# Keeping five transposed K units of batch 0 on chip, lending the wq buffer to the load ring, and turning the q projection round, in a two-layer decode kernel on one core

## The chip, the core and the metric

The kernel runs on one core of one Trainium2 chip. The metric is the time of one execution in microseconds (us) of device time; lower is better. A time is the median of several runs with the lowest and highest beside it. "Span" is the length of one profiled execution, which is 1.5 to 3 us shorter than the time. The ratios given with the times are the mean time of one kernel's fast runs over that of the kernel before in the same rounds, with a 95% interval, so they are not quite the ratio of the medians quoted. By the 2% bar of the record all kernels here are "same" (run 1: "unclear"); "slower" and "faster" below mean only that the interval excludes a ratio of 1.

Words used throughout: PE is TensorE's matmul, PEld its weight load, DVE is VectorE, ACT is ScalarE, SP or SPq the engine (its queue) that issues the loads. L62 is line 62 of that kernel's file. The *granted clock* is the share of TensorE's full speed that the throttle let through. The *DMA share* is the mean busy share of the 16 DMA engines, which can come out a little over 1. A *unit* is 1 MiB of the K or V cache: two chunks of 2048 rows of one head of one batch, 128 x 4096 bf16 on chip. A *slot* is a buffer for one unit.

## The reference, cut to what matters

Two attention layers and two MLPs on one token per batch. **Both layers use the same K and V cache and the same weights.**

```python
# B = 4, D = 512, Hq = 32, Hkv = 8, Sk = 8192, Dh = 128, F = 1792, all bf16
def attn(x, k_cache, v_cache, wq, wo):
    q = (x @ wq).reshape(B, 1, Hq, Dh).transpose(0, 2, 1, 3)
    k, v = jnp.repeat(k_cache, 4, axis=1), jnp.repeat(v_cache, 4, axis=1)
    p = softmax(einsum("bhqd,bhkd->bhqk", q, k) * Dh ** -0.5)
    o = einsum("bhqk,bhkd->bhqd", p, v)
    return o.transpose(0, 2, 1, 3).reshape(B, 1, Hq * Dh) @ wo

x = x + attn(layernorm(x), ...)
x = x + (silu(n @ w_gate) * (n @ w_up)) @ w_down      # n = layernorm(x)
x = x + attn(layernorm(x), ...)                       # layer 2: the same caches
x = x + (silu(n @ w_gate) * (n @ w_up)) @ w_down
```

K and V are 64 units each, and each is wanted in two layers: 256 uses of a unit. A use whose unit is still in a slot from layer 1 needs no load.

## The kernel before

A small planner inside the kernel decides the order of all instructions. Loads are issued by SP in one fixed order, given as a string. `a` loads a V unit for layer 1 (all 64 have one); `b` loads it again for layer 2; `c` stands in place of `b` where the unit **stays in its slot** until layer 2 has used it, and is no load; `K` is the next K unit of the K sequence; the rest are weights. The place of a token also sets the priority of the work on its unit. The three digits are batch, head and half.

```python
ORDER = ("K c241 c230 K x a061 c201 c021 c310 c240 K c110 c100 c101 c311 a021 K wq K c000 c020 wo3 c001 K K K "
         ...
         "b220 b321 b251 b340 b341 b370 b371 b320 b350 b351 b360 b361 ")
NSLOT = 11
NLATE = 3
...
KSEQ = [(0, 0), (0, 1), (1, 0), (0, 2), (1, 1), (0, 3), (1, 2), (1, 3)]   # (layer, batch)
```

A load takes the slot that comes free first, and waits on SP until then. A slot comes free when the matmul that used the unit last has ended. Every K unit gets two transposes on VectorE, in place, before its 32 score matmuls:

```python
def k_pair(u, ld, prio, prev):
    _, l, b, g, cp = u
    for h in range(2):
        def t(h=h):
            ap, key = unit_ap(u, h)
            v = ap.bitcast(mybir.dt.uint32)
            op("dve", lambda e: e.transpose(v, v), reads=[key], writes=[key])
        tr.append(PL.add("dve", 1.23, t, [ld], prio))
    ...                                        # 32 matmuls with the transposed K moving, into banks 0 to 3
    st = PL.add("pe", 1.95, qk, tr + [qd, prev] + (scores_free[0] or []), prio, n=64)
    st.slot_of = u                             # its end frees the slot
```

Between the layers each batch has a chain: output projection, layer norm, MLP, layer norm, then the query of layer 2 in two halves of 16 heads. Here `wq` is stationary and the four columns of x move, in 64 small matmuls a half:

```python
def q_proj(heads, deps, tag):
    ...
    for h in heads:
        for kt in range(KT):
            op("pe", lambda e: e.matmul(ps[:, bk * BW + h * B:bk * BW + (h + 1) * B],
                                        lhsT=wq_sb[:, kt, h * Dh:(h + 1) * Dh],
                                        rhs=xnT[:, kt * B:(kt + 1) * B], ...))
...
for hf in range(2):
    mm = q_proj(range(hf * Hq // 2, (hf + 1) * Hq // 2), [cen, mm], tag)   # 2nd half after the 1st
    out_.append(q_half(b, hf, tag, [mm, qs], prior))                      # scale, spread, place in qpad
```

No score of layer 2 of a batch can run before its query. The V product of most heads is already written in the turned-round form (probabilities stationary, V moving, four 32-column tiles side by side), followed by a 128x256 transpose in PSUM; the last three heads (`NLATE`) are written in a direct form.

## Time and profile before

| Measure | Before |
|---|---|
| Time, median of 4 runs beside the changed kernel | 642.83 us (642.42 to 643.32) |
| Profiled span, mean granted clock | 641.5 us, 0.685 |
| Loads of 1 MiB for K and V | 232 (128 K, 104 V; 24 V uses need none) |
| Read from HBM | 257.17 MB |
| Busy: DVE / PE / ACT | 421.6 / 418.5 / 40.2 us |
| Last landing to the end | 11.2 us |

The prediction below shows the page, the stretches and the chain at the hole. One more view carries the argument: the end of the chain of waits, whose columns are start in us, length in us, and what it was.

```profile
610.92 19.43 DMA pool<-in_A_v_cache_dram
...
630.39 1.03 PE ps L705 x32
```

The last load is issued at 610.92 us, lands at 630.35, and what follows (32 matmuls of the last V unit, output projection, layer norm, MLP) takes to the end of the span and has no load beside it.

I took the DMA rate in stretches of 4 us from 0 to 624 us and summed length x (1 - rate/420), where 420 GB/s is what undisturbed stretches show. The sum of a segment is the time that it lost against that rate, as if nothing had been read for so long. One load of 1 MiB is 1.0486 MB / 420 GB/s = 2.5 us.

| Losses in us, before | 0-140 | 140-168 | 168-200 | 200-280 | 280-340 | 340-540 | 540-572 | 572-624 | sum |
|---|---|---|---|---|---|---|---|---|---|
| | 3.9 | 1.6 | 2.6 | -0.1 | 1.3 | 1.5 | 1.9 | 0.0 | 12.6 |

### The profile page before, as it was taken

The page shows a single profiled execution, that of the slowest core. Times are in us where ns is not written, and L with a number is a line of the kernel's source. Part 1 is how long each engine was busy: PE and PEld are TensorE (multiplying, and loading weights), DVE is VectorE, ACT ScalarE, POOL GpSimd, SP SyncE. Part 2 cuts the span into 40 slices and gives each one's busy share as a digit, 9 for nine tenths or more (in the row PEclk, how much of TensorE's full clock was granted, in tenths as well). Part 3 has the DMA queues.
Part 4 walks back from the last instruction along what each step waited for, and adds up shares of the span by engine and source line. Part 5 has one row for each costly group of instructions (what it writes and reads, how often), then busy time and mean ns, then how long its engine had stood idle before and what let it go on. Part 6 is the DMA issues. An engine that isn't in the chain of part 4 may idle for free.

```text
span 641.5 us, 18860 instructions
## 1 busy us (share of the span) xinstructions
PE 418.5 (65%) x8721; PEld 210.1 (33%) x8721; DVE 421.6 (66%) x740; ACT 40.2 (6%) x106; POOL 1.8 (0%) x8
## 2 busy tenths in 40 slices
PE   0276455656677676578775675777666776876765
PEld 0231131215532242235322242224522254622355
DVE  5278864745289979565686976576487763599722
ACT  1000200003000100000200100000200020000200
POOL 1000000000000000000000000000000000000000
PEclk9995676776576789766577686565676675578675
DMA  8999999999999999999999999999999999999991
GB/s 359 411 417 420 407 419 421 406 413 382 403 369 419 421 420 419 420 420 398 415 411 421 420 417 421 420 412 421 404 403 421 418 422 419 393 398 422 420 418 68
DMA packets 41127, 258.39 MB, mean 403 GB/s; under 512 B 3924, under 2 KB 9816, under 8 KB 10840
## 3 DMA queue, kind: packets, MB, share of 16 engines
q1 hardware_dynamic: 41048, 257.19, 97.8%
q8 instruction: 68, 1.11, 0.7%
q14 instruction: 11, 0.09, 0.0%
HBM read 257.17 MB, written 0.00 MB: 401 GB/s over the span
## 4 chain that ended last, share of the span: by engine, by line
DMA 60%; PE 18%; DVE 15%; SPq 4%; issue 2%; ACT 1%
DMA pool<-in_A_k_cache_dram 34%; DMA pool<-in_A_v_cache_dram 26%; DVE pool L568 8%; PE ps L580 7%; PE ps L720 5%; SPq L92 4%; DVE negm L598 2%; PE ps L460 1%; DVE ps L739 1%; PE ps L758 1%; DVE pp L627 1%; PE ps L638 1%; PE ps L683 1%; PE ps L811 1%; DVE osum L741 1%
## 5 line engine op out<-in xcount | busy, mean ns | idle before, releaser
L568 DVE STREAM_TRANSPOSE pool<-pool 128x1024 uint32<-128x1024 uint32 x256 | 303.4, 1223 | 69.0 <-DMA pool<-in_A_k_cache_dram 62.2
L580 PE MATMUL ps<-pool,qpad 32*32 32x512 bf16 x4096 | 229.4, 528 | 84.6 <-DVE pool L568 82.0
L580 PEld LDWEIGHTS ps<-pool,qpad 32*32 32x32 bf16 x4096 | 67.3, 107 | 220.6 <-DVE pool L568 155.0
L720 PE MATMUL ps<-pool,pp 128*32 128x256 bf16 x1952 | 98.2, 352 | 60.5 <-DMA pool<-in_A_v_cache_dram 47.3
L720 PEld LDWEIGHTS ps<-pool,pp 128*32 128x32 bf16 x1952 | 54.6, 116 | 100.5 <-DMA pool<-in_A_v_cache_dram 67.9
L739 DVE STREAM_TRANSPOSE ps<-ps 128x256 f32<-128x256 f32 x61 | 27.9, 457 | 68.9 <-PE ps L720 68.9
L602 ACT ACTIVATE pp<-ps,negm 128x512 bf16<-128x512 f32 x32 | 21.6, 685 | 336.4 <-DVE negm L598 249.2
L683 PE MATMUL ps<-oT,wo_sb 128*128 128x4 bf16 x640 | 22.8, 166 | 15.4 <-DVE oT L743 10.9
L460 PE MATMUL ps<-xnT,wq_sb 128*128 128x4 bf16 x640 | 18.4, 166 | 19.2 <-DMA wq_sb<-in_A_wq_dram 17.5
L683 PEld LDWEIGHTS ps<-oT,wo_sb 128*128 128x128 bf16 x640 | 20.2, 102 | 28.9 <-DVE oT L743 19.1
L598 DVE TENSOR_REDUCE negm<-ps 128x1 f32<-128x512 f32 x32 | 19.8, 679 | 13.0 <-PE ps L580 13.0
L460 PEld LDWEIGHTS ps<-xnT,wq_sb 128*128 128x128 bf16 x640 | 17.6, 103 | 21.0 <-DMA wq_sb<-in_A_wq_dram 17.6
L638 PE MATMUL ps<-ident,pp 128*128 128x128 bf16 x128 | 14.9, 293 | 9.5 <-DVE pp L627 8.8
L638 PEld LDWEIGHTS ps<-ident,pp 128*128 128x128 bf16 x128 | 11.9, 137 | 14.9 <-DVE pp L627 10.8
L446 ACT ACTIVATE lnv<-var,eps_sb 128x4 f32<-128x4 f32 x10 | 3.0, 297 | 219.3 <-DVE var L441 219.3
L741 DVE TENSOR_REDUCE osum<-ps 128x4 f32<-128x32 f32 x61 | 11.7, 191 | 2.1
L743 DVE TENSOR_TENSOR oT<-osum,invL 128x4 bf16<-128x4 f32 x61 | 10.3, 169 | 2.1
L705 PE MATMUL ps<-pp,pool 128*128 128x4 bf16 x192 | 5.9, 167 | 6.5 <-DMA pool<-in_A_v_cache_dram 6.5
L647 ACT ACTIVATE pp<-ps 128x1024 bf16<-128x1024 bf16 x8 | 8.2, 1024 | 23.9 <-PE ps L638 23.9
L627 DVE TENSOR_SCALAR pp<-pp,alpha 128x512 bf16<-128x512 bf16 x32 | 9.0, 343 | 1.1 <-ACT alpha L620 1.1
L758 PE MATMUL ps<-xnT,wg_sb 128*128 128x4 bf16 x280 | 8.2, 166 | 2.1 <-DVE xnT L435 1.5
L811 PE MATMUL ps<-hT,wd_sb 128*128 128x4 bf16 x280 | 8.5, 166 | 1.1 <-DVE hT L803 0.6
(61 smaller groups left out, 126.7 us busy)
## 6 DMA issues: line engine op xcount, KB each, us to landing
pool<-in_A_k_cache_dram SPq DMA_DIRECT2D x128, 1024.0 KB, 9.6
pool<-in_A_v_cache_dram SPq DMA_DIRECT2D x104, 1024.0 KB, 10.7
wq_sb<-in_A_wq_dram SPq DMA_DIRECT2D x1, 4096.0 KB, 24.0
wo_sb<-in_A_wo_dram SPq DMA_DIRECT2D x4, 1024.0 KB, 18.0
wu_sb<-in_B_w_up_dram SPq DMA_DIRECT2D x2, 896.0 KB, 13.9
wg_sb<-in_B_w_gate_dram SPq DMA_DIRECT2D x2, 896.0 KB, 15.9
wd_sb<-in_B_w_down_dram SPq DMA_DIRECT2D x2, 896.0 KB, 12.4
pp<-in_A_x_dram SPq DMA_DIRECT2D x1, 4.0 KB
```

The source lines that it names most:

```text
L92: ins = self.eng[engname].dma_start(out_ap, in_ap)
L460: op("pe", lambda e: e.matmul(ps[:, bk * BW + h * B:bk * BW + (h + 1) * B], lhsT=wq_sb[:, kt, h * Dh:(h + 1) * Dh], rhs=xnT[:, kt * B:(kt ...
L568: op("dve", lambda e: e.transpose(v, v), reads=[key], writes=[key])
L580: op("pe", lambda e: e.matmul(ps[32 * c:32 * (c + 1), a * BW:(a + 1) * BW], lhsT=qpad[rows, qbuf, es_, g, :], rhs=ap[h][rows, :, es_ // 2, ...
L598: op("dve", lambda e: e.tensor_reduce(negm[:, q, a:a + 1], bank(a), AX.X, ALU.max, negate=True), reads=[f"pb{a}"], writes=[f"negm{q}_{a}"])
L602: op("act", lambda e: e.activation(pblk(q)[:, :, a, :], bank(a).rearrange("p (t j) -> p t j", j=32), ACTF.Exp, bias=negm[:, q, a:a + 1], s ...
L627: op("dve", lambda e: e.tensor_scalar(seg, seg, alpha[:, q, a:a + 1], None, op0=ALU.mult), reads=[f"pp{q}_{a}", f"alpha{q}"], writes=[f"pp ...
L638: op("pe", lambda e: e.matmul(stg[:, t * P:(t + 1) * P], lhsT=pp[:, q, blk * P:(blk + 1) * P], rhs=ident[:], is_transpose=True, start=True ...
L683: op("pe", lambda e: e.matmul(ps[:, OPJ * BW + nq * B:OPJ * BW + (nq + 1) * B], lhsT=wo_sb[:, h, nq * P:(nq + 1) * P], rhs=oT[:, l, h, :], ...
L720: op("pe", lambda e: e.matmul(ps[32 * n:32 * (n + 1), bk * BW:bk * BW + 256], lhsT=pp[:, q, col:col + 32], rhs=v[:, 8 * f:8 * (f + 1), 32 ...
L739: op("dve", lambda e: e.transpose(blk, blk), reads=[f"pb{bk}"], writes=[f"pb{bk}"])
L741: op("dve", lambda e: e.tensor_reduce(osum[:], diag, AX.X, ALU.add), reads=[f"pb{bk}"], writes=["osum"])
```

## The change

Its intent: (1) keep the last five transposed K units of batch 0's layer 1 in their slots, so that layer 2 of batch 0 needs neither load nor transpose for them and can score as soon as its query is there; (2) hand the `wq` buffer (four units long) to the load ring as four more slots once the last query is projected; (3) project the query with x stationary and `wq` moving, four 32-column tiles side by side, 16 matmuls a half; (4) load the last unit in two halves, so that half of its matmuls run before the last landing; (5) a new load order, in which batch 0 keeps no V unit (before 6) and batches 1 to 3 keep 6, 5 and 7 (before 6 each). Besides, the K units of a batch come in another order of heads, and the step lengths that the planner assumes were set anew, so that the order of all instructions differs.

```diff
+            for i in range(s.gives):
+                slots.append((s.end + self.HOP, self.nslots + i))
...
-NLATE = 3
+LATE = (6, )
+KM = (5, 0, 0, 0)
+TAILSPLIT = True
...                                               (the order string is replaced)
+        def q_rows(hf, deps, tag):
+            nh = Hq // 2
+            def mm():
+                bk = pbk(tag)
+                for kt in range(KT):
+                    w = wq_sb[:, kt, hf * nh * Dh:(hf + 1) * nh * Dh].rearrange("p (h d) -> p h d", d=Dh)
+                    for n in range(4):
+                        op("pe", lambda e: e.matmul(ps[32 * n:32 * n + B, bk * BW:(bk + 1) * BW],
+                                                    lhsT=xnT[:, kt * B:(kt + 1) * B],
+                                                    rhs=w[:, :, 32 * n:32 * (n + 1)],
+                                                    start=(kt == 0), stop=(kt == KT - 1), tile_position=(0, 32 * n)),
...                                               (in q_half)
-                src = ps[:, bass.ds(bk * BW + b + hf * nh * B, nh, step=B)]
+                blk = bank(bk).bitcast(mybir.dt.uint32)
+                op("dve", lambda e: e.transpose(blk, blk), reads=[f"pb{bk}"], writes=[f"pb{bk}"])
+                src = ps[:, bass.ds(bk * BW + b, nh, step=32)]
...
+        def slot_sb(s):
+            return pool[:, s, :] if s < NSLOT else wq_sb[:, s - NSLOT, :]
...                                               (in load_pair: the last unit in two loads)
+            return [PL.load(1.25, lambda: half(0), u), PL.load(1.25, lambda: half(1), None)]
...                                               (in k_pair)
-            for h in range(2):
+            for h in range(2 if ld is not None else 0):
...
-            st.slot_of = u
+            if u not in kept_k:
+                st.slot_of = home[u]
...                                               (in the chain)
-                mm = q_proj(range(hf * Hq // 2, (hf + 1) * Hq // 2), [cen, mm], tag)
+                mm = q_rows(hf, [cen, mm], tag)
                 out_.append(q_half(b, hf, tag, [mm, qs], prior))
+            if b == B - 1:
+                mm.gives = KT
...                                               (in the load loop)
-                loads[u] = load_pair(u)
+                if u[1] == 1 and ("k", 0) + u[2:] in kept_k:
+                    home[u] = ("k", 0) + u[2:]
+                else:
+                    loads[u] = load_pair(u)
```

## The prediction

> **What bounds the kernel now.** I read the page's first four parts first, then the stretches (rate of the DMA engines, 4 us at a time over the whole span), then the chain of waits and the DMA queue's own waits around each dip.
>
> From the page: engine totals, two of the rows in 40 slices, DMA queue, chain.
>
> ```profile
> PE 418.5 (65%) x8721; PEld 210.1 (33%) x8721; DVE 421.6 (66%) x740; ACT 40.2 (6%) x106; POOL 1.8 (0%) x8
> ...
> DMA  8999999999999999999999999999999999999991
> GB/s 359 411 417 420 407 419 421 406 413 382 403 369 419 421 420 419 420 420 398 415 411 421 420 417 421 420 412 421 404 403 421 418 422 419 393 398 422 420 418 68
> ...
> q1 hardware_dynamic: 41048, 257.19, 97.8%
> ...
> DMA 60%; PE 18%; DVE 15%; SPq 4%; issue 2%; ACT 1%
> ```
>
> No compute engine passes 66%. The 16 DMA engines are busy from the first slice to the last but one, and most slices sit at 419 to 422 GB/s. So the kernel is bound by bytes: 257.17 MB at 420 GB/s are 612 us of a span of 641.5. The other 29 us are a start, a tail without loads, and the dips. The stretches size these (columns: stretch, length, busy us of PE, PEld, DVE, ACT, POOL, granted clock, DMA share, GB/s):
>
> ```profile
> 0.00:4.00 4.00, 0.00 (x0) 0.00 (x0) 0.22 (x2) 1.28 (x1) 1.84 (x8) 1.00 0.56 164
> 144.00:160.00 16.00, 10.09 (x210) 7.86 (x194) 9.05 (x35) 4.86 (x13) 0.00 (x0) 0.61 1.06 381
> 172.00:180.00 8.00, 4.92 (x140) 3.66 (x144) 3.18 (x8) 0.00 (x0) 0.00 (x0) 0.50 0.72 273
> 288.00:300.00 12.00, 10.38 (x210) 5.50 (x202) 8.54 (x28) 0.00 (x0) 0.00 (x0) 0.56 0.99 388
> 456.00:460.00 4.00, 2.67 (x50) 1.77 (x49) 2.27 (x8) 1.29 (x4) 0.00 (x0) 0.63 0.93 358
> 544.00:552.00 8.00, 7.46 (x176) 5.61 (x173) 4.44 (x18) 0.42 (x2) 0.00 (x0) 0.50 0.94 376
> 560.00:568.00 8.00, 6.83 (x138) 2.06 (x128) 6.83 (x9) 0.00 (x0) 0.00 (x0) 0.70 0.99 375
> 184.00:224.00 40.00, 26.68 (x484) 7.85 (x470) 36.93 (x36) 2.06 (x7) 0.00 (x0) 0.71 1.01 421
> 572.00:624.00 52.00, 36.88 (x785) 18.88 (x769) 35.59 (x63) 4.11 (x10) 0.00 (x0) 0.70 1.01 420
> 628.00:642.00 14.00, 8.23 (x254) 7.49 (x251) 3.14 (x16) 0.75 (x3) 0.00 (x0) 0.50 0.03 11
> ```
>
> Loss of a stretch = length x (1 - rate/420). That gives 2.4 us for the start; 1.5 at 144 to 160, where the share is 1.06, so the engines are not idle but busy with weight loads of short rows; 2.8 at 172 to 180, the one real hole (share 0.72); then 0.9, 0.6, 0.8 and 0.9. The five losses after the weights sum to 6.0 us, and are the most that better slots can give back. The last two data stretches matter for the change: from 572 to 624 us the rate is already 420, with 11 slots.
>
> The hole has a cause in the DMA queue's own waits from 160 to 185 us:
>
> ```profile
> SPq L62 <- PE ps L720: 22.4, 5, 9.7
> SPq L62 <- PE ps L580: 3.5, 2, 2.0
> ```
>
> The queue waits for V units to be consumed (L720), once for 9.7 us. In the chain of waits these V matmuls come only at 176.63, behind the query path of batch 0 that starts at 168.61:
>
> ```profile
> 169.74 1.88 PE ps L460 x64
> ...
> 171.93 1.88 PE ps L460 x64
> 173.84 0.25 DVE qT L523
> ...
> 176.36 0.23 DVE qpad L533
> ...
> 176.63 1.93 PE ps L720 x24
> ...
> 183.04 8.29 DMA pool<-in_A_k_cache_dram
> ```
>
> **What the Trainium skill says.** "HBM Reference", section Specifications: a core streaming alone measures about 425 GB/s, bounded by its 16 DMA engines. The trace agrees with 420. "Perfetto Trace Analysis", section Identifying the Most-Contended Engine: improve that engine, and for TensorE busy time is no measure. Here it is the DMA, so work taken from VectorE is worth something only where it frees a slot earlier. "TensorEngine Tiling (Array Packing)", section Performance Considerations: with a moving operand of at most 32 columns, swap stationary and moving operand and tile the columns four ways. That is what the new q projection does. The V product already has this form: 16 matmuls of 128x256 take 1.04 us at clock 0.5 and 0.62 us at full clock in the trace.
>
> **The change part by part.**
>
> *Bytes.* In the order string I counted layer-2 V loads that are skipped: 24 before, 18 after. K loads: 128 before, 123 after, for the five units kept transposed. So 232 loads of 1 MiB become 233: the change loads one MiB more. At 1.0486 MB / 420 GB/s that is +2.5 us on the bound resource, certain.
>
> *VectorE.* Kept K units save 5 x 2 transposes x 1.223 us = 12.2 us. The new q path adds a 128x512 PSUM transpose for each of 8 halves: the 128x256 one measures 0.457 us, so I estimate 0.8 to 0.9, together 7. Only one late V group is direct instead of three, so two more 128x256 transposes with sums, 2 x 0.8. VectorE goes from 422 to about 418 us: nothing on its own.
>
> *TensorE.* A half of the projection is 64 matmuls in 1.87 us now; after it is 16 of 128x512, by the V rows twice 0.62 to 1.04, so 1.2 to 2.0 us. With the added transpose the query path stays about as long (6.9 us now, 169.74 to 176.59). No gain there by itself; PE does not bind.
>
> *Slots.* I worked out from the two instruction orders how many MiB lie between the newest unit that must be consumed before a load gets its slot and that load (the lookahead). Before, it is 3 to 4 at loads 65 to 91, 110 to 147, 165 to 204 and from 213 on (5 to 10 between), with two 2s at loads 213 and 218, which by their bytes are at 545 to 565 us: the dips at 544 and 560. A K unit's loop without queueing is about 2 us latency (an estimate: the last landing at 630.35 against the end of bytes near 628.4, as the last stretch of 14 us at 11 GB/s holds 0.4 us of full rate), 2.5 transfer, two transposes 2.38, matmuls 1.95: 8.9 us. A lookahead of 4 means five loads in the loop, 12.5 us. So 4 suffices, as 421 GB/s at 184 to 224 shows, and 3 just does (10 us), unless a query or softmax chain stands between.
>
> After: in the stage from load 64 to 88, where the hole is, lookahead is 5 to 10 instead of 3 to 4, because the first five K units of layer 2 need no load and are scored as soon as q is there; the loads before them are V units and no longer wait on the units stuck behind the query path. I take 2.5 of the 2.8 us as regained. From load 177 to 203 it is 5 instead of 4 (worth 0.3 at the dip of 456). In the last K stage the four wq slots take it from 4 to 7; but there the rate was 420 already, so only the dip of 560 to 568 is to be had: 0.7. At loads 112 to 121 and 211 to 217 it is 3, as before, so the dips of 288 and 544 stay.
>
> The price: five slots stay occupied while batch 1 is scored. There the lookahead falls from 5 to 8 down to 4 or 5, and to 3 at one load near 54 MiB. I put +0.7 us for small new dips.
>
> *Tail.* The last landing is at 630.35, the span ends at 641.5. The last unit now comes in two halves, so after the last landing 16 instead of 32 matmuls remain: half of 1.03, -0.5 us. The rest of the tail (projection, MLP, transpose out) is unchanged.
>
> Sum: +2.5 - 2.5 - 0.3 - 0.7 + 0.7 - 0.5 = -0.8 us. From 642.7 that is 641.9. An order that was searched anew with the load time set by measurement (2.495 for 2.515) may avoid a bit more of the remaining 2.5 us of dips; I take another -0.9 and predict 641.0.
>
> **The rivals.** First, bytes alone: the holes move instead of closing, and the time is 642.7 + 2.5 - 0.5 = 644.7. For it: the stage of batch 1 has fewer free slots. Against it: the hole at 172 has one named cause that the kept units remove. Second, all dips close: 642.7 + 2.5 - 6.0 - 0.5 = 638.7, the floor unless the rate itself rises. Against it: two dips keep a lookahead of 3. Third, VectorE is the hidden limit (transposes end 8% of the chain) and its relief gives several us: 636. Against it: in 184 to 224 us VectorE is 92% busy and the DMA still runs at 421. Fourth, the kept K starve the stage of batch 1, with a new hole as large as the old one: 646. The softmax of batch 1 falls there, and lookahead 4 leaves only 3.6 us of slack in the K loop.
>
> **Range and chances.** The floor of 638.7 and the two bad cases of 644.7 and 646 frame it: 638.0 to 645.0 eight times in ten, with 641.0 as the value. 2% are 12.9 us, more than twice all dips together, so faster by over 2% (under 629.8) would need bytes to vanish: 0.01. Slower by over 2% needs holes of 10 us: 0.015. Within 2%: 0.975.
>
> **What would show it.** HBM read 258.2 MB; 246 in place of 256 K transposes, and 8 new 128x512 PSUM transposes of under 1 us. No stretch of 8 us under 350 GB/s between 160 and 190 us; 420 GB/s at 560 to 568. About 10.6 us from the last landing to the end. Dips of 0.5 to 1 us remaining near 290 to 310 and 545 to 555. I am wrong if a stretch between 100 and 160 us shows a share well under 1, if the rate of the clean stretches differs from 420, or if VectorE's saving shows up as time.

## The result, and the profile after

| | Before | After |
|---|---|---|
| Time, median of 4 runs each | 642.83 us (642.42 to 643.32) | 642.87 us (642.66 to 643.85) |
| Ratio after / before | | 1.0003, interval 0.9986 to 1.0021 |
| Profiled span, clock | 641.5 us, 0.685 | 641.0 us, 0.665 |
| HBM read | 257.17 MB | 258.22 MB |
| DVE busy | 421.6 us | 415.1 us |

The time is the same. The page after:

```profile
PE 419.1 (65%) x8273; PEld 202.0 (32%) x8273; DVE 415.1 (65%) x742; ACT 40.2 (6%) x106; POOL 1.8 (0%) x8
...
GB/s 343 422 418 406 404 417 420 420 413 402 400 395 421 421 419 420 422 419 399 410 393 422 421 420 419 421 419 420 419 421 420 418 421 414 386 420 422 418 419 84
...
DMA 69%; PE 19%; DVE 8%; SPq 2%; issue 1%; ACT 0%
```

TensorE has 448 instructions fewer, VectorE is 6.5 us less busy, 1.05 MB more are read, and 23 of the 40 slices sit at 419 to 422 GB/s (20 before, where the prediction says "most"). The chain is still made of loads. Now the stretches that answer to those of before (stretch, length, busy us of PE, PEld, DVE, ACT, POOL, granted clock, DMA share, GB/s):

```profile
172.00:180.00 8.00, 4.66 (x108) 3.39 (x108) 1.67 (x9) 0.00 (x0) 0.00 (x0) 0.50 1.01 420
...
186.00:194.00 8.00, 7.65 (x224) 3.75 (x218) 5.05 (x6) 0.00 (x0) 0.00 (x0) 0.65 0.89 366
288.00:300.00 12.00, 10.66 (x228) 6.10 (x226) 8.75 (x27) 0.25 (x1) 0.00 (x0) 0.50 1.00 399
...
324.00:332.00 8.00, 6.34 (x121) 2.40 (x129) 7.83 (x7) 0.00 (x0) 0.00 (x0) 0.74 0.98 370
456.00:460.00 4.00, 2.08 (x32) 0.91 (x32) 1.15 (x4) 0.32 (x1) 0.00 (x0) 0.50 1.02 420
544.00:552.00 8.00, 7.89 (x217) 6.29 (x218) 3.74 (x18) 0.75 (x3) 0.00 (x0) 0.50 0.99 368
560.00:568.00 8.00, 6.26 (x112) 1.79 (x97) 8.00 (x8) 0.00 (x0) 0.00 (x0) 0.57 1.01 422
...
572.00:624.00 52.00, 35.43 (x726) 17.35 (x726) 35.89 (x67) 4.10 (x10) 0.00 (x0) 0.75 1.01 420
```

The holes of before at 172 to 180 (273 GB/s), 456 (358) and 560 to 568 (375) are gone. New are a smaller one at 186 to 194 and one at 324 to 332; the dip of 544 to 552 stays. The same sums as before, with the difference:

| Losses in us | 0-140 | 140-168 | 168-200 | 200-280 | 280-340 | 340-540 | 540-572 | 572-624 | sum |
|---|---|---|---|---|---|---|---|---|---|
| before | 3.9 | 1.6 | 2.6 | -0.1 | 1.3 | 1.5 | 1.9 | 0.0 | 12.6 |
| after | 4.4 | 1.3 | 1.1 | 0.0 | 2.2 | 0.2 | 1.3 | 0.0 | 10.5 |
| after - before | +0.5 | -0.2 | -1.5 | 0.0 | +0.9 | -1.3 | -0.6 | 0.0 | -2.2 |

So the reads lose 2.2 us less and take 2.5 us more for one more MiB. The last landing is at 630.35 us in the trace of before and at 630.30 in that of after. What remains is the tail:

```profile
178.76 0.65 PE ps L432 x2
...
179.89 1.91 PE ps L481 x16
...
181.82 0.74 DVE ps L544
...
182.88 1.91 PE ps L481 x16
...
186.78 1.83 PE ps L617 x29
...
630.35 0.60 PE ps L743 x16
```

The last line answers to the 32 matmuls in 1.03 us of before: 16 matmuls in 0.60 after the last landing. From last landing to the end are 10.7 us, 0.45 less. The other lines are the query path of batch 0: layer norm at 178.76, each half a projection of 1.91 us and a transpose of 0.74 us on VectorE, first score of layer 2 at 186.78. Before, the layer norm began at 168.61, ten microseconds earlier. In both orders TensorE waits for two V units just ahead of it (the second lands at 176.67, before at 166.52), so that is not what is new. Most of the delay is there already at the layer norm that opens the MLP, before and then after:

```profile
156.61 0.64 PE L426 MATMUL ps<-xx,onesm 128*128 128x32 f32 x2 [0.78 <-DVE pp L649]
163.24 0.64 PE L432 MATMUL ps<-xx,onesm 128*128 128x32 f32 x2 [1.00 <-DVE oT L789]
```

The new order issues the last piece of `wo` at 139.58 us (before 131.58) and the last piece of the MLP's weights at 157.85 (before 149.64); run 6 below moves these weights and the last V unit of batch 0 forward, and the norm ahead of the query comes 8 us earlier. The first score of layer 2 is later by less, 186.78 against 181.09, because before the change V products were put between the query and that score. The DMA does not stop while the query path is late, as the units loaded meanwhile have slots. It stops later, at 188 us, when SP waits for the first scores. The DMA queue's own waits from 160 to 195 us (who waits, for whom, us in total, times, longest):

```profile
SPq L92 <- PE ps L617: 13.8, 5, 10.5
SPq L62 <- PE ps L758: 10.5, 5, 6.7
```

Before it was a V matmul (L720) that the queue waited for longest, here it is a score of layer 2 (L617), 10.5 us in one wait.

### The profile page after: what moved, and what is told of

Same layout as the page of the kernel before. It is cut to its first block, busy times and chain, and to the rows that moved or that the text cites. A ratio compares the mean times of both kernels' runs of the same rounds, so it can differ in the third digit from the quotient of the medians.

```text
span 641.0 us, 17956 instructions
## 1 busy us (share of the span) xinstructions
PE 419.1 (65%) x8273; PEld 202.0 (32%) x8273; DVE 415.1 (65%) x742; ACT 40.2 (6%) x106; POOL 1.8 (0%) x8
## 3 DMA queue, kind: packets, MB, share of 16 engines
q8 instruction: 64, 1.05, 0.7%
HBM read 258.22 MB, written 0.00 MB: 403 GB/s over the span
## 4 chain that ended last, share of the span: by engine, by line
DMA 69%; PE 19%; DVE 8%; SPq 2%; issue 1%; ACT 0%
DMA pool<-in_A_v_cache_dram 31%; DMA pool<-in_A_k_cache_dram 25%; PE ps L617 7%; PE ps L758 6%; DVE pool L605 5%; DMA wq_sb<-in_A_v_cache_dram 5%; DMA wq_sb<-in_A_wq_dram 4%; SPq L92 2%; DMA wq_sb<-in_A_k_cache_dram 2%; DMA wo_sb<-in_A_wo_dram 2%; PE ps L481 2%; PE ps L804 1%; PE ps L857 1%; DVE ps L785 1%; PE ps L721 1%
## 5 line engine op out<-in xcount | busy, mean ns | idle before, releaser
L605 DVE STREAM_TRANSPOSE pool<-pool 128x1024 uint32<-128x1024 uint32 x232 | 273.9, 1221 | 68.2 <-DMA pool<-in_A_k_cache_dram 64.0
L617 PE MATMUL ps<-pool,qpad 32*32 32x512 bf16 x3872 | 215.3, 535 | 70.9 <-DVE pool L605 61.0
L758 PE MATMUL ps<-pool,pp 128*32 128x256 bf16 x1920 | 102.5, 368 | 74.0 <-DMA pool<-in_A_v_cache_dram 59.8
L617 PEld LDWEIGHTS ps<-pool,qpad 32*32 32x32 bf16 x3872 | 66.4, 108 | 192.8 <-DVE pool L605 118.3
L636 DVE TENSOR_REDUCE negm<-ps 128x1 f32<-128x512 f32 x32 | 19.8, 680 | 10.4 <-PE ps L617 10.4
L605 DVE STREAM_TRANSPOSE wq_sb<-wq_sb 128x1024 uint32<-128x1024 uint32 x14 | 16.4, 1217 | 2.9 <-DMA wq_sb<-in_A_k_cache_dram 2.6
L481 PE MATMUL ps<-wq_sb,xnT 128*4 128x512 bf16 x128 | 13.3, 565 | 2.4 <-DVE qT L546 2.3
L617 PE MATMUL ps<-wq_sb,qpad 32*32 32x512 bf16 x224 | 10.5, 439 | 3.8 <-DVE wq_sb L605 3.6
L804 PE MATMUL ps<-xnT,wu_sb 128*128 128x4 bf16 x280 | 8.8, 166 | 2.3 <-DVE oT L789 1.1
L544 DVE STREAM_TRANSPOSE ps<-ps 128x512 uint32<-128x512 uint32 x8 | 5.7, 715 | 7.0 <-PE ps L481 7.0
L758 PE MATMUL ps<-wq_sb,pp 128*32 128x256 bf16 x96 | 5.7, 384 | 6.7 <-DMA wq_sb<-in_A_v_cache_dram 6.7
## 6 DMA issues: line engine op xcount, KB each, us to landing
wq_sb<-in_A_v_cache_dram SPq DMA_DIRECT2D x7, 1024.0 KB, 16.3
```

Source lines behind the costliest of these rows:

```text
L481: op("pe", lambda e: e.matmul(ps[32 * n:32 * n + B, bk * BW:(bk + 1) * BW], lhsT=xnT[:, kt * B:(kt + 1) * B], rhs=w[:, :, 32 * n:32 * (n + ...
L617: op("pe", lambda e: e.matmul(ps[32 * c:32 * (c + 1), a * BW:(a + 1) * BW], lhsT=qpad[rows, qbuf, es_, g, :], rhs=ap[h][rows, :, es_ // 2, ...
L636: op("dve", lambda e: e.tensor_reduce(negm[:, q, a:a + 1], bank(a), AX.X, ALU.max, negate=True), reads=[f"pb{a}"], writes=[f"negm{q}_{a}"])
L758: op("pe", lambda e: e.matmul(ps[32 * n:32 * (n + 1), bk * BW:bk * BW + 256], lhsT=pp[:, q, col:col + 32], rhs=v[:, 8 * f:8 * (f + 1), 32 ...
L804: op("pe", lambda e: e.matmul(ps[:, bk * BW + (fo - f0) * B:bk * BW + (fo - f0 + 1) * B], lhsT=w_sb[:, kt, fo * P:(fo + 1) * P], rhs=xnT[: ...
```

## The experiments

My theory after the result: **the time is bytes plus holes; one load is 2.5 us; the change pays one load and buys 2.2 us of holes and 0.45 us of tail with it, and the parts of the change are worth what they do to these two.** Rivals: VectorE's or TensorE's work sets the time; or the parts do nothing at all. Each run was a set of three rounds (five for the last), every one gave the correct result, and the edit is against the changed kernel. The kernel before measured 642.6 to 642.9 us in all of them; the changed kernel was not run again. After each edit the planner orders all instructions anew, so a run differs from the changed kernel in more than the line shown.

### 1. No K unit kept

```diff
-KM = (5, 0, 0, 0)
+KM = (0, 0, 0, 0)
```

> The changed kernel with the five K units of batch 0 loaded again for layer 2: 238 instead of 233 loads of 1 MiB, ten more K transposes, and five slots more in circulation while batch 1 is scored. Bytes theory (the DMA engines at 420 GB/s set the time): +5 x 2.5 us = +12.5 us over the changed kernel, less up to 1 us if the added slots close a dip, so 654 to 656 us. Rival (the kept units matter through VectorE and slots, and a load more is hidden in the dips): within 2 us of 642.9.

Measured: 655.34 us (655.12 to 655.69), ratio 1.0183 (1.0159 to 1.0207). That is 12.5 us above the changed kernel, and five loads are 5 x 2.5 = 12.5. The losses to 624 us are 9.95 us, 0.5 less than after: no hole at 188 (0.2 us in 168 to 200), but 2.7 in 280 to 340. So the kept K units count by the bytes they save, and they cost a small hole (the first score is as late here, 187.46 us, but more slots circulate). The relief of VectorE, which would also be lost here (ten transposes), leaves no mark beside the bytes.

### 2. Keeping one V unit of batch 0 as well

The unit V of batch 0, head 2, second half is loaded early for layer 1 and again for layer 2 in the changed kernel. Keeping it saves one load, so that the number of loads is again that of before, 232.

```diff
-  ... a170 a171 a120 b021 K K K c320 K "
+  ... a170 a171 a120 c021 K K K c320 K "
```

> The changed kernel, with one more V unit (batch 0, group 2, second half) kept on chip between the layers instead of being loaded again early and waiting: 232 loads, as before the change; the lookahead falls by one or two at a few loads near 58 to 66 MiB, once to 2.9. Bytes theory: -2.5 us and perhaps +0.3 from a new dip, so 640.1 to 641.0 us. Rival (the dips of the changed kernel come from its chains and absorb a load): 642.5 to 643.

Measured: 643.12 us, ratio 0.9992 (0.9973 to 1.0012). The theory missed: the saved 2.5 us did not come. The stretch that the loss comes from, and the queue's longest wait in 165 to 195 us:

```profile
180.00:188.00 8.00, 6.54 (x152) 2.61 (x145) 3.74 (x9) 0.00 (x0) 0.00 (x0) 0.60 0.68 248
```

```profile
SPq L92 <- PE ps L617: 17.9, 5, 15.4
```

One slot fewer circulates, so the ring is full earlier and SP waits 15.4 us for the first score instead of 10.5. The losses in 168 to 200 rise from 1.1 to 3.5 us and in 140 to 168 from 1.3 to 2.5: 3.6 together, more than the load saved, of which 0.9 comes back in 280 to 340. My reading of what the theory lacked: **before a fixed point (the first score), a load saved is a load's time of hole, because the slots are full anyway.** Against this run, the extra MiB of the change is free where it stands: it fills the hole.

### 3. The query projection of before

```diff
-                mm = q_rows(hf, [cen, mm], tag)
+                mm = q_proj(range(hf * Hq // 2, (hf + 1) * Hq // 2), [cen, mm], tag)
 (and in q_half the PSUM transpose is left out and the old column stride put back)
```

> The changed kernel with the layer-2 q projection as before (weights stationary, 64 matmuls a half, no transpose on VectorE), all else kept. My theory: at the granted clock of 0.5 both forms of a half take 1.88 us on TensorE, and the new one adds 0.73 us of transpose behind it, so the query path is no shorter with the new form and bytes hide it: 642.3 to 643.2 us, no difference over 0.3 us. Rival (the new form shortens the path that ends the dips): the old form costs 1 to 3 us, 644 to 646.

Measured: 644.71 us (643.7 to 645.85), ratio 1.0017 (0.9993 to 1.0042). 1.8 us slower in the median than the changed kernel, which the interval does not settle: it includes no difference. In the trace of batch 0 the old form takes the same time a half (64 matmuls in 1.88 us against 16 in 1.91), both at a granted clock of 0.5. Not so in batch 2, where the new form ran at a clock of 0.84 to 1.00 (436 to 444 us) and the old one at 0.50, after and then run 3:

```profile
437.62 1.03 PE L481 MATMUL ps<-wq_sb,xnT 128*4 128x512 bf16 x16
436.06 1.86 PE L466 MATMUL ps<-xnT,wq_sb 128*128 128x4 bf16 x64
```

The old form gains little from the clock: at 1.00, in 28 to 32 us of the trace of before, 128 such small matmuls take 3.57 us, 1.8 for 64. The hole at 188 us is a little smaller in run 3 (0.7 in 168 to 200; the first score comes at 184.97), as no PSUM transpose stands in the path. It loses elsewhere: 0.9 against 0.2 us in 340 to 540, and in the query path of batch 3 the chain has two pieces of "issue" (time in which the engine waited for nothing that the profile shows), 0.63 and 0.94 us, that the changed kernel's chain does not have there; the first slot of the `wq` buffer is asked for at 558.57 us instead of 556.87. The losses to 624 us differ by only 0.3, yet the last landing comes at 631.53 us, 1.2 later. So the new form may be worth up to some 2 us; neither this nor where it would come from is shown.

### 4. and 5. The wq slots: none, and one

```diff
-                mm.gives = KT
+                mm.gives = 0        # run 4 (11 slots in the last stage)
+                mm.gives = 1        # run 5 (12 slots)
```

> The changed kernel without the four slots in the region of wq: the last stage runs on 11 slots, lookahead 3 (twice 2) instead of 7 over the last 25 loads. My theory: a K unit's loop of 8.9 us fits into four loads of 2.5 us, so little is lost, 0.5 to 1.5 us (the dip at 560 to 568 us comes back): 643.4 to 644.4 us. Rival (the last stage needs deeper lookahead, 3 is starvation): 646 us or more, with several stretches under 400 GB/s after 560 us. Second rival (slots of wq are worth nothing): 642.9.

> The changed kernel with one slot in the region of wq instead of four: lookahead 4 in the last stage; it was 7 with four slots (642.9 us) and 3 with none (650.6 us). My theory (before the change, 4 held 420 GB/s; the knee lies between 3 and 4): 642.8 to 644.0 us, no stretch of 8 us under 400 GB/s after 568 us. Rival (each slot buys some, all four are needed): 646 to 648 us.

Measured: with none 650.63 us (649.89 to 651.94), ratio 1.0111 (1.0088 to 1.0134); with one 643.52 us (643.06 to 644.23), ratio 1.0014 (1.0 to 1.0029); with four it was 642.87. With none, by my reading of the instruction orders, three loads lie between the newest unit that must be consumed and the load that gets its slot (the lookahead), with one it is four, with four seven. The prediction's "3 just does" is refuted: 7.8 us. (It made an exception for a query or a softmax in between: of the 9.0 us that the losses to 624 us rise, 2.9 come in 540 to 572, around the query path, but 6.1 in 572 to 624.) The stretches without the slots, then the second one with one slot (run 5):

```profile
560.00:564.00 4.00, 2.93 (x56) 0.81 (x49) 4.00 (x5) 0.00 (x0) 0.00 (x0) 0.64 0.61 209
...
576.00:612.00 36.00, 22.86 (x367) 6.61 (x352) 24.44 (x32) 2.96 (x9) 0.00 (x0) 0.55 0.94 350
```

```profile
576.00:612.00 36.00, 24.19 (x418) 10.05 (x418) 27.44 (x49) 4.10 (x10) 0.00 (x0) 0.67 1.01 420
```

The chain without the slots:

```profile
564.94 7.19 DMA pool<-in_A_k_cache_dram
...
572.16 2.38 DVE pool L605 x2
...
574.58 1.95 PE ps L617 x31
...
576.59 7.43 DMA pool<-in_A_k_cache_dram
```

One turn of the loop is 576.59 - 564.94 = 11.65 us: 7.2 from issue to landing, two transposes 2.38, the scores 1.95 at a clock of 0.5. Four loads are issued in a turn, so one load takes 2.9 us instead of 2.5, over the whole last stage. The prediction had 8.9 us for the turn (its terms sum to 8.8), with about 2 us latency and 2.5 of transfer. That the 7.2 us are longer because a load is issued behind three others and shares the engines with them is my reading; no run separates it. With a lookahead of four there are five loads in a turn, and the rate is 420 again in 576 to 612 us. The kernel before had a lookahead of 3 to 4 here by the same reading and lost nothing in 572 to 624; it kept one V unit of batch 3 less in its 11 slots. Counted by slots: 11 less 7 kept are 4 that circulate without `wq` (run 4), 5 with one slot (run 5), 8 with four, and 11 less 6 were 5 before.

### 6. and 7. The weights of the MLP earlier, with and without the kept V unit

Since the query path of batch 0 starts late, the order was changed so that the last V unit of batch 0's layer 1 and the weights of the MLP come ahead of five V units of batch 1 (the expectation says six).

```diff
-  wo2 a161 a060 a160 a110 wd1 c100 a111 wu1 wd0 a170 a171 a120 b021
+  wo2 a060 wu1 wd1 wd0 a161 a160 a110 c100 a111 a170 a171 a120 b021     # run 6
+  wo2 a060 wu1 wd1 wd0 a161 a160 a110 c100 a111 a170 a171 a120 c021     # run 7
```

> The changed kernel with the same 233 loads, but the last V unit of layer 1, batch 0, and the three pieces of the MLP weights moved ahead of six V units of batch 1, so that the query path of batch 0 can end about 10 us earlier. My theory now (the hole near 185 us lasts from the last load that needs no slot freed by a score of layer 2 until the query path of batch 0 is through): the query path ends near 175 us instead of 187, and the 0.9 us lost at 188 to 192 us are gone: 641.7 to 642.5 us, no stretch under 390 GB/s between 172 and 200 us. Rival (the hole comes from too few slots, whatever the query path does): no change, 642.9.

> Early weights as in early_w, and the V unit of keep_v021 kept on chip: 232 loads. In keep_v021 the load saved came back as a hole of 3.3 us at 180 to 188 us. My theory: with the query path done early the hole is at most 1 us and the saved load shows: 639.8 to 641.0 us, faster than both kernels. Rival (a saved load is always given back): 642.5 to 643.2.

Measured: 645.0 us (643.91 to 645.67), ratio 1.0035 (1.002 to 1.005); and 644.34 us, ratio 1.0032 (1.0015 to 1.0048). Both missed, and both are slower. The first step did happen: the layer norm ahead of the query came at 170.82 us instead of 178.76, and the first score of layer 2 at 178.8 instead of 186.78 (run 6). But the hole came earlier too, and larger; the two stretches, run 6 then run 7:

```profile
176.00:188.00 12.00, 10.44 (x272) 5.16 (x272) 3.07 (x10) 0.00 (x0) 0.00 (x0) 0.74 0.80 304
```

```profile
176.00:184.00 8.00, 6.54 (x136) 2.44 (x128) 2.24 (x7) 0.00 (x0) 0.00 (x0) 0.50 0.40 147
```

The losses in 168 to 200 us are 3.3 and 5.2 us, against 1.1. The V units of batch 1 now land while TensorE runs the chain, and hold the slots until it is done; the queue waits 10.5 us for a V matmul and 10.5 us for a score in run 6. So starting the chain earlier moved the point at which every slot is full, as I read it, and did not remove it.

### 8. The same, and one more V unit of batch 3 kept

```diff
-  ... b331 b350 b351 b310 b330 b370 b371 b360 b361
+  ... b331 b350 b351 b310 b330 b370 b371 c360 b361      (on top of run 7)
```

> early_w_keep1 with one more V unit kept, of batch 3 (group 6, first half): 231 loads, but the lookahead is 2 instead of 3 at five loads that fall near 545 to 556 us, around the query path of batch 3. Bytes alone would give 2.5 us more, 637.5. I expect most of it to come back as a hole there, 1.5 to 2.5 us: 639 to 640.6 us. Rival (lookahead 2 is harmless there): 637.5 to 638.5.

Measured: 644.72 us, ratio 1.0036 (1.0021 to 1.0051). One load less than run 7 and no time won: 540 to 560 us falls to 334 GB/s, 4.1 us lost, at a lookahead of 2 (540 to 572 lost 1.5 in run 7).

```profile
540.00:560.00 20.00, 16.27 (x352) 10.72 (x348) 10.47 (x41) 1.25 (x5) 0.00 (x0) 0.56 0.90 334
```

The second kept unit is given back in another stage, in the same way.

### 9. A sixth K unit kept

```diff
-KM = (5, 0, 0, 0)
+KM = (6, 0, 0, 0)
```

> The changed kernel with six K units of batch 0 kept instead of five: 232 loads, two transposes fewer, one slot fewer in circulation until the query path of batch 0 is through. My theory (a sixth kept unit of batch 0, K or V, saves a load of 2.5 us and loses as much in the hole before the first score of layer 2, as the kept V unit did): a hole of 2.5 to 3.5 us between 175 and 192 us instead of 0.9, and 642.4 to 643.4 us. Rival (K is better to keep than V, since it saves VectorE as well): 640.4 to 641 us.

Measured: 646.23 us (645.36 to 647.24), ratio 1.0049 (1.003 to 1.0067), 3.4 us slower with one load less.

```profile
128.00:160.00 32.00, 19.34 (x322) 9.82 (x325) 16.42 (x37) 4.11 (x10) 0.00 (x0) 0.50 0.94 357
...
188.00:196.00 8.00, 6.54 (x168) 2.82 (x168) 3.79 (x6) 0.00 (x0) 0.00 (x0) 0.55 0.63 249
```

The hole at 188 to 196 was expected. The dips of 128 to 160 were not: there batch 1 is scored with six slots taken, at a lookahead of 2 to 3 by my reading of the order. Together the losses to 624 us are 16.3 us against 10.5. Of 0, 5 and 6 kept units five is the fastest in this order, which was searched for five (4 was not tried); my prediction's rival of a starved batch 1 is what the sixth unit brings, not the fifth.

### 10. and 11. Two scores between the halves of the query

The first two K units of layer 2 belong to heads whose query is in the first half. Here they are scored before the second half is projected, so that two slots come free some 4 us earlier. Run 11 also keeps the V unit of run 2.

```diff
-                mm = q_rows(hf, [cen, mm], tag)
+                mm = q_rows(hf, [cen, out_[0]] if hf else [cen], tag)
...
-                st = k_pair(u, loads.get(u), prio[u], st)
+                st = k_pair(u, loads.get(u), [-20.0 + n] if l == 1 and n < 2 else prio[u], st)
...
-  ... a120 b021 K K K                 (run 11 alone)
+  ... a120 c021 K K K
```

> The changed kernel with the two halves of each layer-2 query taken apart: the first two K units, which need only the first half, are scored before the second half is projected. Same 233 loads. In the changed kernel the first score of batch 0 starts at 186.7 us, 6.8 us after the projection begins. My theory (the hole ends with that score): it starts 3 us earlier, the 0.9 us at 188 us go, and perhaps 0.5 us at the query paths of the other batches: 641.4 to 642.3 us. Rival (slots, not the query path): 642.9, or slower if the second half is late.

> Query halves taken apart as in split_q2, and the V unit of keep_v021 kept: 232 loads. In keep_v021 the hole was 3.3 us, at 180 to 188 us, with the first score at 183.4. My theory: the first score starts near 180.2 us, the hole shrinks to 0.5 to 1.5 us, and part of the saved load shows at last: 640.5 to 641.8 us, faster than both kernels. Rival (every saved load comes back as a hole): 642.5 to 643.3.

Measured: 647.33 us, ratio 1.0063 (1.0044 to 1.0082); and 646.66 us, ratio 1.0052 (1.0036 to 1.0069). Both slower, and yet both did at batch 0 what they were made for. The losses in 168 to 200 us are 0.2 us in run 10 (1.1 after) and 0.9 in run 11 (3.5 in run 2). In run 11, 213.9 MiB are read by 544 us, against 214.2 in the changed kernel, which has one MiB more to read: 0.7 MiB ahead, 1.8 us. Then both lose it in batch 3, run 10 and then run 11:

```profile
560.00:568.00 8.00, 7.02 (x152) 2.26 (x154) 5.44 (x7) 0.00 (x0) 0.00 (x0) 0.58 0.51 172
```

```profile
556.00:568.00 12.00, 6.90 (x176) 2.48 (x176) 9.52 (x14) 0.00 (x0) 0.00 (x0) 0.70 0.58 212
```

In batch 3 the second half of the query is what frees the `wq` buffer. Put behind two scores, it frees it late: the first loads into it go out at 556.91 us in the changed kernel, at 566.64 in run 10 and at 564.67 in run 11 (start, us to the last issue, loads):

```profile
556.91 1.75 SPq L92 DMA_DIRECT2D wq_sb<-in_A_k_cache_dram  x4
566.64 2.67 SPq L92 DMA_DIRECT2D wq_sb<-in_A_k_cache_dram  x4
564.67 1.78 SPq L92 DMA_DIRECT2D wq_sb<-in_A_k_cache_dram  x4
```

The losses in 540 to 572 us are 6.7 and 7.4 us, against 1.3.

### 12. The scores between the halves in batches 0 to 2 only, and the V unit kept

```diff
-  [cen, out_[0]] if hf else [cen]                                (against run 11)
+  [cen, mm] if b == B - 1 else [cen, out_[0]] if hf else [cen]
...
-  [-20.0 + n] if l == 1 and n < 2 else prio[u]
+  [-20.0 + n] if l == 1 and b < B - 1 and n < 2 else prio[u]
```

> The changed kernel with the early V load of batch 0 (the unit for v021) kept on chip again (one load of 1 MiB fewer, 232 as before the change) and with the first two score units of layer 2 placed between the two halves of the query projection, in batches 0 to 2 only; batch 3 as in the changed kernel. Theory (the reads are what the time is made of, and a saved load counts only where no hole opens for it): the run that did this in all four batches was 0.7 MiB (some 1.8 us) ahead of the changed kernel by 544 us and lost it at 556 to 568 us, where the second half in batch 3 freed the wq slots late. Without that in batch 3 the loss should go: 640.6 to 641.8 us, a ratio to the kernel before of 0.9965 to 0.9985, the hole of 180 to 188 us below 1 us, and no stretch of 4 us below 350 GB/s in 556 to 568. Rival (the saved load is always given back later, since scoring in batches 1 to 3 is what sets the pace): 642.5 to 644 us, with new dips somewhere in 200 to 540 us. Second rival (the loss of 556 to 568 us came from the earlier reads themselves, as the slots fill up sooner, and not from the split in batch 3): a dip of over 3 us stays at 556 to 568 and the time is 645 us or more.

Measured: 641.75 us (641.2 to 642.9, 5 runs), ratio 0.9977 (0.9963 to 0.9991). As the theory has it:

```profile
180.00:188.00 8.00, 7.39 (x176) 2.71 (x176) 3.15 (x5) 0.00 (x0) 0.00 (x0) 0.62 0.94 373
...
560.00:568.00 8.00, 5.26 (x128) 1.89 (x127) 8.00 (x8) 0.00 (x0) 0.00 (x0) 0.90 1.02 424
```

The hole of batch 3 is gone, which settles that the split in batch 3 made it and not the earlier reads; that it did so by way of the late `wq` buffer is what the trace says (here it is loaded from 555.68 us on). The hole of 180 to 188 lost 0.9 us, as expected, against 3.3 in run 2. What else is lost goes in 140 to 168 (2.4 us, where run 11 lost the same) and in 340 to 540 (1.1, against 0.2), so a part of the saved load is given back, as the rival says. The trace is that of the slowest of the five runs. It is 1.2 us faster than the kernel before in the median, and the interval excludes a ratio of 1. Against the changed kernel, by way of the kernel before, it is 0.9977 / 1.0003, about 0.3% faster, and the two intervals still touch.

All the loss sums side by side, which is the evidence that the argument rests on:

| Kernel | loads | losses 140-168 | 168-200 | 280-340 | 340-540 | 540-624 | sum to 624 | time |
|---|---|---|---|---|---|---|---|---|
| before | 232 | 1.6 | 2.6 | 1.3 | 1.5 | 1.9 | 12.6 | 642.83 |
| after | 233 | 1.3 | 1.1 | 2.2 | 0.2 | 1.3 | 10.5 | 642.87 |
| 1 no kept K | 238 | 1.3 | 0.2 | 2.7 | 0.2 | 1.3 | 9.9 | 655.34 |
| 2 V unit kept | 232 | 2.5 | 3.5 | 1.3 | 0.3 | 1.5 | 13.7 | 643.12 |
| 3 old projection | 233 | 1.2 | 0.7 | 2.2 | 0.9 | 1.3 | 10.7 | 644.71 |
| 4 no wq slots | 233 | 1.3 | 1.0 | 1.7 | 0.6 | 10.4 | 19.4 | 650.63 |
| 5 one wq slot | 233 | 1.2 | 1.2 | 1.8 | 0.4 | 2.2 | 11.2 | 643.52 |
| 6 early weights | 233 | 1.4 | 3.3 | 1.1 | 0.3 | 1.7 | 12.6 | 645.00 |
| 7 the same, V unit kept | 232 | 1.4 | 5.2 | 1.0 | 0.4 | 1.5 | 14.1 | 644.34 |
| 8 the same, two kept | 231 | 1.4 | 5.1 | 1.3 | 0.2 | 4.0 | 16.7 | 644.72 |
| 9 six K kept | 232 | 3.5 | 3.9 | 1.3 | 0.2 | 1.6 | 16.3 | 646.23 |
| 10 scores between | 233 | 1.2 | 0.2 | 1.6 | 1.0 | 6.6 | 15.4 | 647.33 |
| 11 the same, V unit kept | 232 | 2.4 | 0.9 | 1.2 | 0.8 | 7.3 | 16.9 | 646.66 |
| 12 last version | 232 | 2.4 | 1.8 | 1.2 | 1.1 | 1.3 | 12.4 | 641.75 |

Check it against the changed kernel: run 1 is 5 x 2.5 - 0.6 = +11.9 us by the table and +12.5 measured; run 9 is 5.8 - 2.5 = +3.3 and +3.4; run 10 is +4.9 and +4.5; run 4 is +8.9 and +7.8. Every run agrees to about a microsecond but run 3, which is +0.3 by the table and +1.8 measured, and stays open: rates are rounded, and traces differ between executions.

## Why the prediction came out as it did

The value was 641.0 us, 1.9 below what was measured, with a range of 7 us that held it; a range so wide beside a change of nothing is no proof of the working. The mechanism stood (a load more against smaller holes), and several terms of its sum were mis-sized, partly against each other.

- **Bytes, +2.5: right.** HBM read was 258.22 MB as expected, there were 14 + 232 = 246 K transposes, and run 1 shows five loads as 12.5 us.
- **The hole at 172 to 180, -2.5: the largest miss among the holes.** It is gone where it was, and no stretch of 8 us between 160 and 190 is below 350 GB/s. But 168 to 200 as a whole went from 2.6 to 1.1 us, so 1.5 were regained. The step that failed is the assumption that V units in place of stuck ones close the hole. The ring fills up behind the first score as well. The query path did stay as long as I said (some 7 us from the first projection until the query is in place), but it starts 10 us later, which the prediction did not consider.
- **The dip at 456, -0.3: too small.** 340 to 540 us went from 1.5 to 0.2, as the dip at 468 (0.6) went too. I had not listed it, so this gain is luck.
- **The dip at 560 to 568, -0.7: right**, -0.6 in 540 to 572. The reason given was incomplete: I called 3 sufficient, and run 4 shows that in this stage 3 costs 7.8 us and 4 almost nothing. The slots of `wq` are what the seventh kept V unit of batch 3 needs, not a bonus; this follows from the count of slots, as no run kept six units without them.
- **New small dips, +0.7: at the wrong place.** Before 168 us, where I put them, the sum is +0.3 (the start +0.5, 140 to 168 -0.2). A dip of 1.0 at 324 to 332 was not in the sum, and 280 to 340 lost 0.9 more than before. Kernels that lose less ahead of 200 us tend to lose more here (2.7 in run 1, 2.2 after, 1.3 in runs 2 and 9), as if reads that are early run into the pace of the scores. That is argued from the table, not tested by a run.
- **The tail, -0.5: right** by the two traces, 11.15 to 10.7 us; no run undid the halves of the last unit alone.
- **The further -0.9 for a searched order: unfounded.** No view carried it, and nothing shows it. Without it, the sum was 641.9, 1.0 from the result. A hope was entered as a term.
- **VectorE's relief, 0: right.** 6.5 us less busy (I had worked out some 4), no time; a sixth kept K unit relieves it further (run 9) and is slower.
- **The query projection, no gain by itself: right in duration in batch 0** (1.91 us for 1.88 in a half; in batch 2, at a higher clock than before, 1.03 for 1.86), open in effect: run 3 is 1.8 us slower in the median with an interval that includes 0.

Of the four rivals, bytes alone (644.7) is refuted, as 2.2 us of holes did close; all dips closed (638.7) and the VectorE limit (636) are refuted by the time. Starvation of batch 1 (646) did not come with five units and came with six (run 9: 646.23).

So the expected gain was not lost to one thing. It was **given back**: the change frees 2.7 us (holes 2.2, tail 0.45) and spends 2.5 on a load. And in runs 2, 7, 8 and 9 simply dropping a load did not bank it: the losses rose in the stages where the kept unit takes a slot. One rival is not tested: the order was searched for the changed kernel's own settings, and a run that changes one of them keeps this order. Run 12 shows that a part can be banked when the scores are moved too; a new search for each setting might bank more.

## What to carry to other kernels

In a kernel that is bound by its reads and fed from a ring of slots, a unit kept on chip saves one load and takes one slot; whether it pays is decided in the stage with the fewest free slots and the next fixed point (here the first score after a chain), so read the DMA queue's own waits there before keeping more. Here it was better to fill such a hole with a load that is wanted later (run 2) than to start the chain ahead of it earlier (run 6). Count a loop's turn with loads that queue behind each other (7.2 us from issue to landing here, not 4.5). Sum the losses by stage before and after: a hole that closed at one address may stand a few microseconds further on.

## What the Trainium skill lacked or had wrong

- "TensorEngine Tiling (Array Packing)", section Performance Considerations, advises the swap with fourfold column tiling for a small moving operand. At a granted clock of 0.5 it gave no time here: 64 small matmuls take 1.88 us and 16 tiled ones of 512 columns 1.91 us; in batch 2, at a clock of 0.84 to 1.00, the tiled ones take 1.03 us. The turned-round form adds a 0.74 us transpose in PSUM. Another page fits the first: "TensorE: Matmul & The Clock Gate", section Wait — 56ns, not 53.3ns?, states 426.7 ns from start to start for 512 columns with the array cold. An estimate from that page: 4 rounds of four side by side are 1.71 us, which the 1.91 here agree with. The first page could say that the swap wins nothing here at half clock, where 64 small matmuls pass in 1.88 us.
- No page that I read says how many loads must be under way in a ring of buffers. In this case's last stage a lookahead of 3 gives 650.63 us, 4 gives 643.52 and 7 gives 642.87, with 11.65 us for a turn of four loads of 1 MiB.
- "DMA: Bandwidth & Descriptors", section Specifications, gives 512 B as the least size for the full rate. The trace of before shows 381 GB/s in 144 to 160 us with the engines busy at a share of 1.06, while weights are loaded among the units, and 2638 of its 3494 packets are under 2 KB but only 99 under 512 B (a row of `wo` or w_down is 1 KB); clean stretches, without weights, are at 420. So a stretch with many rows of 1 KB did not reach the full rate here; that the rows are the reason is likely, but no run changed their length. The point is that table row alone: elsewhere the skill does count an overhead for small descriptors.
